# Late weight steps three products later, and scores in tiles of 64 rows in four periods: an attention and feed-forward kernel on one core

## The chip, the core and the metric

The kernel runs on one core of one Trainium2 chip. A core has TensorE (PE, matrix products into PSUM; its weight loads are listed as PEld), VectorE (DVE), ScalarE (ACT), GpSimd (POOL) and SyncE (SP, which issues most DMAs). The metric is the device time of one execution in microseconds (us). All inputs and outputs lie in the chip's memory, and one launch computes everything.

## What is computed

Attention in which a query sees only the keys of its own cluster, and then a feed-forward block (ffn) over all tokens:

```python
# q, k, v: (4, 8, 768, 64); centroids: (8, 16, 64); all float32
q_assign = argmax(einsum('bhsd,hcd->bhsc', q_n, c_n), -1)      # the same for k; _n: normalised
mask     = q_assign[:, :, :, None] == k_assign[:, :, None, :]
scores   = where(mask, q @ k.T / sqrt(64), -1e9)
scores   = scores - max(scores, -1)
attn     = exp(scores); attn = attn / (sum(attn, -1) + 1e-9)
x        = (attn @ v), heads side by side: (3072, 512)

h  = x @ w_in                       # w_in: (512, 2048)
sp = maximum(h, 0) + log1p(exp(-abs(h)))
g  = h * erf(sp)
out = g @ w_out                     # w_out: (2048, 512); out: (3072, 512)
```

## The kernel before

**Attention.** Two heads make a pair `p` (16 pairs), one head on partitions 0 to 63 and one on 64 to 127. A pair has two halves of 384 queries and six blocks of 128 keys; a unit `u` is one half against one block of keys, 12 units a pair, 192 in all. The loop at the bottom calls `period(p, i)` 96 times, each for two units. A period issues in order: a step of the maxima for the coming half (`step_ahead(u)`), `products(u)` and `products(u + 1)`, a second step of the maxima in two pieces, `scores(u)`, `scores(u + 1)`, the exponentials (`curve`) on ACT, and for the two units of the period before the sums (`accumulate`) on POOL and the product with v (`attend`) on PE. At the start of every half stands `divide` for the half before: row sums by a product with `minus`, Ln and Exp on ACT, four DVE instructions, and four DMAs to `x_dram`.

`products` multiplies q and k (float32, 64 rows of contraction for each head, and so two row tiles of the array at a time). `scores` adds onto the same PSUM tile what masks and shifts: `qm` and `km` hold, in bfloat16, a one-hot of the cluster and, in row 0 of each head, the negated maximum. Rows 32 to 63 of each head hold the one-hot of the cluster again. `scores` uses rows 0 to 31 of each head, that is, tiles of 32 rows at rows 0 and 64; the second step of the maxima in a period (`behind=True`) uses rows 32 to 63 and 96 to 127, in tiles of 32 rows as well. Maxima are taken one half ahead: `step_ahead(u)` works for unit `u + 6`. So none is left for the last six units (186 to 191, three periods), and in the first period (`u == 0`) they are issued ahead of the period and after its scores.

**The ffn.** A matrix product is done as seven smaller ones over sums and differences of the quarters of its operands ("forms": `left_forms`, `right_forms`). `hidden(n, lot)` makes one half of h for the chunk `n` of 512 tokens: four blocks of seven products, each product of 4 matmul records into a PSUM bank of its own, evicted by the functions that `fresh` lists. Of a block, product 1 is copied by ACT (`first=ae.copy`) and products 2, 6, 7, 5 (twice), 3 and 4 are taken by DVE, in this order. `block` runs, after each product and its evictions, the next `pace` entries of a list `aside_work`, which holds single instructions of other work in the order in which they are to be issued; `finish_aside` issues what is left at the end. Program order is kept on PE, DVE, ACT and POOL.

The banks: six of the pool `psb`, in turn; from the end of the first block on (`finish_attention`, which runs the last `divide`) also the two `turned` tiles of attention, as the seventh and eighth of every eight products.

**The weights.** Each weight step takes 512 columns of a weight matrix, already fetched as 512 KB, and turns them into a float32 array in five parts: `size_and_rest` (ACT, two instructions), `bounded` (DVE), `sign` (ACT), `shifted` (DVE) and `summed` (POOL). `summed` also issues the fetch that uses the freed place. The last ten steps (`N_LATE`, all of `w_out`) run in the ffn. Their first four fetches are issued ahead of `hidden(0, 0)`, into memory that attention held until its last accumulation. Steps 0 to 3 are run beside `hidden(0, 0)` (28 products, `pace` 1, 20 parts), followed by eight POOL instructions that make forms of `w_out` (`out_forms[0]`, `out_forms[1]`); steps 4 to 9 beside `hidden(0, 1)`, together with the gate (softplus and erf on ACT, product on DVE).

Of the kernel before, what the change touches and what calls it, by code (L numbers as in the profile page):

```python
# [20 lines left out]
B, H, S, D = 4, 8, 768, 64  # L21
C = 16
NJ = S // P
Q = 32
# [46 lines left out]
def kernel(  # L71
# [68 lines left out]
    rows = [{nm: const.tile([P, S], F32, name=f"{nm}T{i}") for nm in "qk"} for i in range(2)]  # L140
# [124 lines left out]
    for e in range(2):  # L265
        for n in range(2):
            r = e * D + n * Q
# [50 lines left out]
    def similarities(p):  # L318

        if p >= NPAIR:  # L320
            return
        st = pairs[p]
        st["psim"] = turned[1][:, 0:HW]
        for g in range(4):
            te.matmul(
                st["psim"][2 * C * g : 2 * C * (g + 1)], lhsT=ccT[:, p % HP],
                rhs=st["qk"[g // 2] + "T"][:, (g % 2) * HW : (g % 2 + 1) * HW],
                start=True, stop=True,
            )
# [31 lines left out]
    def masks(p, nm, half, bank, narrow=False, copied_by=ae):  # L361

        if p >= NPAIR:
            return lambda: None
        st = pairs[p]
        cols = slice(half * HW, (half + 1) * HW)
        r, hot = slice(0, D) if nm == "q" else slice(D, P), st["hotT"]
        picked = pick[r, half]
        if narrow:
            r = slice(r.start + Q, r.stop)  # L370
            picked = pick[r, 1]
            hot = hot if half else st["aside"]
        won = bank[:, 0:HW]
        te.matmul(won, lhsT=picked, rhs=hot[r], start=True, stop=True)
        if nm == "q":
            return lambda: ae.activation(out=st["qm"][:, cols], in_=won, func=ACT.Relu)
        if copied_by is ve:
            return lambda: ve.tensor_scalar(
                out=st["km"][:, cols], in0=won, scalar1=BIG, scalar2=nbig, op0=ALU.mult, op1=ALU.add
            )  # L380
        return lambda: ae.activation(
            out=st["km"][:, cols], in_=won, func=ACT.Identity, bias=nbig, scale=BIG
        )
# [34 lines left out]
    def turn(p, h, copies=(ae.copy, ae.copy)):  # L418

        st = pairs[p]  # L420
        pn = turned[h][:, 0:HW].rearrange("p (t n) -> p t n", t=HJ)
        for t in range(HJ):
            for e in range(2):
                cols = slice(e * D, e * D + Q)
                te.matmul(pn[cols, t], lhsT=lowest[h][:, t, cols], rhs=identb, start=True, stop=True)
        for e, copy in zip(range(2), copies):
            r = slice(e * D, e * D + 1)
            copy(out=st["qm"][r, h * HW : (h + 1) * HW], in_=pn[r].rearrange("p t n -> p (t n)"))
        st["shift", h] = True
# [4 lines left out]
    units = [(p, half, j) for p in range(NPAIR) for half in range(2) for j in range(NJ)]  # L434
# [3 lines left out]
    def products(u):  # L438
        p, half, j = units[u]
        if u in sc_of:  # L440
            return
        st = pairs[p]
        sc = sc_of[u] = ps_s.tile([P, 2, 512], F32, name="sc", tag="s")
        for e in range(2):
            r = slice(e * D, (e + 1) * D)
            te.matmul(
                sc[:, e, 0:HW], lhsT=st["kT"][r, j * P : (j + 1) * P],
                rhs=st["qT"][r, half * HW : (half + 1) * HW], start=True, stop=False,
            )

    def scores(u):

        p, half, j = units[u]
        st = pairs[p]
        sc = sc_of[u]
        assert ("shift", half) in st
        for e in range(2):
            r = slice(e * D, (e + 1) * D)
            r = slice(r.start, r.start + Q)
            te.matmul(  # L460
                sc[:, e, 0:HW], lhsT=st["km"][r, j * P : (j + 1) * P],
                rhs=st["qm"][r, half * HW : (half + 1) * HW], start=False, stop=True,
            )

    def curve(u):

        pr = prs[u % NPT]
        sc = sc_of.pop(u)[:, :, 0:HW].rearrange("p e (c x) -> p e c x", c=2)
        ae.activation(out=pr[:, :, :, 0:QW], in_=sc, func=ACT.Exp, scale=D**-0.5)
# [143 lines left out]
    aside_work = []  # L613
# [89 lines left out]
    def idle(n):  # L703
        return [lambda: None] * n
# [39 lines left out]
    def run(work):  # L744
        for _ in work:
            pass
# [3 lines left out]
    def step_ahead(u, behind=False):  # L750
        p, i = divmod(u + NJ, 2 * NJ)
        steps = maxima_step(p, i, behind=behind) if p < NPAIR else iter(())
        if not behind:
            run(steps)
        return steps
# [7 lines left out]
    def period(p, i):  # L763
        u = 2 * NJ * p + 2 * i
        n1, n2 = 2 * p - 1, 2 * p
        early = lambda n: 0 <= n < N_EARLY

        def mask(place):
            which = (MASKS if p else FIRST_MASKS).get((i, place))
            if which:  # L770
                return masks(p + 1, *which, turned[0 if i in (0, 5) else 1], place > 1, ve if i == 0 else ae)
            return lambda: None

        if u > 0:
            for which in turns if i in (0, 3) else ():
                turn(*which)
                turns.remove(which)
            step_ahead(u)
        mask(0)()
        next(part[0], None)  # L780
        if i == 5:
            next(routing[0], None)
        if i == 0 and p:
            run(routing[0])
        if u == 2:
            next(routing[0])
        products(u)
        products(u + 1)
        mask(1)()
        second = step_ahead(u + 1, True) if u > 0 else iter(())  # L790
        next(second, None)
        scores(u)
        next(second, None)
        if i:
            next(second, None)
        next(part[0], None)
        scores(u + 1)
        later = mask(2)
        if i == 0:
            later()  # L800
            later = lambda: None
            next(second, None)
        if i == 3:
            similarities(p + 2)
            routing[0] = choose(p + 2, sc_of[u + 1][:, 0], True)
        curve(u)
        later()
        curve(u + 1)
        if u == 0:
            step_ahead(1)  # L810
            similarities(1)
            routing[0] = choose(1, turned[0])
            next(routing[0])
            next(routing[0])
            vectors(1, "q")
            vectors(1, "k")
        if i == 0 and early(n1 - 1):
            bounded(n1 - 1)
            shifted(n1 - 1)
            sign(n1 - 1)  # L820
        elif i == 1 and early(n1):
            size_and_rest(n1)
        elif i == 3 and early(n1):
            bounded(n1)
            sign(n1)
        elif i == 5 and early(n2):
            rest(n2)
        for _ in range(min(len(forms), FORMS.get(p, {}).get(i, 0))):
            forms.pop(0)[0]()
        if i == 3:  # L830
            next(routing[0], None)
            if early(n1):
                shifted(n1)
            for _ in range(2):
                next(routing[0], None)
        elif i == 1:
            load(p + 1, "v", v, vp)
            if p == 0:
                run(routing[0])
                transposes(2, "q")  # L840
        elif i == 2:
            transposes(p + 2, "k")
        elif i == 4:
            vectors(p + 2, "k")
            vectors(p + 2, "q")
        elif i == 5:
            transposes(p + 3, "q")
        if u > 0:
            if i == 1 and early(n1 - 1):
                summed(n1 - 1)  # L850
            elif i == 4 and early(n1):
                summed(n1)
            for w in (u - 2, u - 1):
                accumulate(w)
            if i % HJ == 1 and p in POOL_FORMS and forms:
                forms.pop(0)[1]()
            for w in (u - 2, u - 1):
                attend(w)
            if i % HJ == 0:
                part[0] = divide(u - 1)  # L860
                next(part[0])
        if i == 3 and early(n2):
            size(n2)
# [71 lines left out]
    u = len(units)  # L935
# [30 lines left out]
    def all_weights(lo, hi):  # L966
        return sum((weights(n) for n in range(lo, hi)), [])

    out_forms = [right_forms(ge, *w_out_parts(f, 2)) for f in range(0, HF, 2)]
# [10 lines left out]
            del a[:1], b[:1]  # L980
        return work

    aside_work += all_weights(0, 4) + out_forms[0] + out_forms[1]
    hidden(0, 0, {0: finish_attention})
    finish_aside()
    aside_work += together(idle(2) + gates(0, 0, (0,)), all_weights(4, N_LATE))
# [56 lines left out]
```

## Time and profile before

Three runs took 995.52, 995.58 and 996.94 us; the median is 995.58. The profiled execution took 995.37 us, and its span, from the first instruction to the last, is 993.7 us.

| what | value |
|---|---|
| attention, from the start to the last product with v on PE | to 408.4 us |
| first ffn step, `hidden(0, 0)`, PE | 408.4 to 434.5 us |
| second ffn step, `hidden(0, 1)`, PE | 434.5 to 458.65 us |
| busy of DVE, ACT, POOL in 408.4 to 435.3 (26.90 us) | 19.36, 14.24, 13.40 us |
| busy of DVE, ACT, POOL in 435.3 to 458.6 (23.30 us) | 21.15, 18.11, 10.38 us |
| score passes of 32 rows, 384 columns: number, mean | 384, 326 ns |
| DMA landing of a late weight step (512 KB), median | 3.3 us (into `g_more`), 4.7 us (into `osb`) |

In the lists of the profile a line gives the start, the duration, the engine, the operation with output and inputs by their names in the program, the tile of the array (`64*128` is 64 rows by 128 columns), the shape, and the number of instructions that were put together; in brackets stands how long the engine had been idle and what ended that. The end of a matmul is modelled, so two starts are compared rather than an end and a start. A matmul in float32 appears as two records. All instructions bear one line number (L62), since a helper issues them, so the tile names tell them apart. `sc` is the tile of products and scores, `wide` that of the maxima, `bank` an ffn bank.

### The profile page before, as it was taken

The page shows a single profiled execution, that of the slowest core. Times are in us where ns is not written, and L with a number is a line of the kernel's source. Part 1 is how long each engine was busy: PE and PEld are TensorE (multiplying, and loading weights), DVE is VectorE, ACT ScalarE, POOL GpSimd, SP SyncE. Part 2 cuts the span into 40 slices and gives each one's busy share as a digit, 9 for nine tenths or more (in the row PEclk, how much of TensorE's full clock was granted, in tenths as well). Part 3 has the DMA queues.
Part 4 walks back from the last instruction along what each step waited for, and adds up shares of the span by engine and source line. Part 5 has one row for each costly group of instructions (what it writes and reads, how often), then busy time and mean ns, then how long its engine had stood idle before and what let it go on. Part 6 is the DMA issues. An engine that isn't in the chain of part 4 may idle for free.

```text
span 993.7 us, 20557 instructions
## 1 busy us (share of the span) xinstructions
PE 985.4 (99%) x8362; PEld 738.8 (74%) x8362; DVE 708.4 (71%) x1361; ACT 488.2 (49%) x659; POOL 350.6 (35%) x237
## 2 busy tenths in 40 slices
PE   8999999999999999999999999999999999999998
PEld 3555555555555555688888888888888888888887
DVE  8888888888888886779676564756475647655653
ACT  3777777777776665575432414150505050505050
POOL 1688888787888888562400000000000000000000
PEclk9999999999999999999999999999999999999999
DMA  9444444444444210321000100010001000000001
GB/s 220 83 109 109 111 112 112 110 114 110 93 88 108 51 34 18 114 97 61 1 22 22 43 1 22 22 43 1 22 22 43 1 21 22 1 1 22 22 1 42
DMA packets 147294, 55.88 MB, mean 56 GB/s; under 512 B 128640, under 2 KB 137088, under 8 KB 147200
## 3 DMA queue, kind: packets, MB, share of 16 engines
q1 hardware_dynamic: 144848, 54.29, 21.5%
q8 instruction: 65, 1.06, 0.4%
q10 hardware_dynamic: 2352, 0.30, 0.2%
q14 instruction: 29, 0.24, 0.1%
HBM read 41.98 MB, written 12.58 MB: 55 GB/s over the span
## 4 chain that ended last, share of the span: by engine, by line
PE 95%; DVE 1%; POOL 1%; DMA 1%; issue 0%; SPq 0%; ACT 0%; ACTq 0%; DVEq 0%; POOLq 0%
PE bank L62 43%; PE turned L62 31%; PE sc L62 16%; PE wide L62 6%; POOL more_out L62 1%; DVE nmx L62 1%; DMA g_more<-in_moe_w_out_dram 0%; DMA in_k<-in_k_dram 0%; SPq L62 0%; DMA in_q<-in_q_dram 0%; DVE kT L62 0%; DVE sims L62 0%; POOL x_more L62 0%; DVE qT L62 0%; ACT pr L62 0%
## 5 line engine op out<-in xcount | busy, mean ns | idle before, releaser
L62 POOL TENSOR_TENSOR more_out<-more_out,pr 128x768 f32<-128x768 f32 x128 | 217.2, 1697 | 18.6 <-ACT pr L62 10.1
L62 DVE TENSOR_REDUCE nmx<-wide 128x2 f32<-128x768 f32 x189 | 180.5, 955 | 48.2 <-PE wide L62 47.2
L62 ACT ACTIVATE pr<-sc 128x768 f32<-128x768 f32 x192 | 148.9, 812 | 94.6 <-PE wide L62 78.6
L62 PE MATMUL turned<-pr,in_v 128*32 128x194 f32 x3072 | 145.5, 330 | 0.0
L62 PEld LDWEIGHTS turned<-pr,in_v 128*32 128x32 f32 x3072 | 91.5, 109 | 51.2 <-issue 21.3
L62 DVE TENSOR_TENSOR g<-bank,g 128x256 f32<-128x256 f32 x222 | 89.7, 422 | 52.9 <-PE bank L62 46.3
L62 PE MATMUL bank<-x_own,w_in 128*128 128x256 f32 x424 | 104.7, 380 | 0.9 <-DVE g L62 0.9
L62 PE MATMUL bank<-w_out,g 128*128 128x256 f32 x448 | 103.1, 379 | 0.0
L62 PE MATMUL sc<-qT,kT 64*128 64x384 f32 x528 | 98.3, 486 | 0.0
L62 PEld LDWEIGHTS bank<-w_out,g 128*128 128x128 f32 x448 | 85.1, 190 | 11.6
L62 PEld LDWEIGHTS bank<-x_own,w_in 128*128 128x128 f32 x424 | 80.3, 190 | 12.7 <-DVE g L62 1.3
L62 DVE TENSOR_TENSOR osb<-bank,osb 128x256 f32<-128x256 f32 x87 | 35.5, 421 | 72.8 <-ACT osb L62 25.4
L62 ACT COPY g<-bank 128x256 f32<-128x256 f32 x28 | 10.4, 372 | 152.9 <-PE bank L62 148.4
L62 ACT ACT_TABLE_LOAD x48 | 61.6, 1283 | 45.7 <-DVE g L62 45.1
L62 PE MATMUL bank<-x_more,more_in 128*128 128x256 f32 x296 | 76.0, 379 | 0.0
L62 POOL TENSOR_TENSOR more_out<-pr,pr 128x768 f32<-128x768 f32 x32 | 60.1, 1879 | 28.1 <-ACT pr L62 28.1
L62 PEld LDWEIGHTS <-qv 64*128 64x128 bf16 x384 | 26.9, 93 | 53.1 <-issue 37.0
L62 PEld LDWEIGHTS sc<-qT,kT 64*128 64x128 f32 x528 | 50.0, 187 | 21.3 <-ACT inv L62 2.3
L62 PE MATMUL wide<-kv,qv 64*128 64x384 bf16 x378 | 64.0, 328 | 1.3 <-DVE nmx L62 0.6
L62 PE MATMUL bank<-more_out,g_more 128*128 128x256 f32 x272 | 64.3, 379 | 0.0
L62 DVE TENSOR_TENSOR g<-a_s,g 128x512 f32<-128x512 f32 x96 | 62.5, 689 | 1.4 <-ACT a_s L62 1.4
L62 PE MATMUL wide<-km,qm 64*128 64x384 bf16 (+1 forms) x378 | 62.5, 327 | 0.0
(172 smaller groups left out, 1669.9 us busy)
## 6 DMA issues: line engine op xcount, KB each, us to landing
x_own<-in_moe_w_in_dram SPq DMA_DIRECT2D x13, 512.0 KB, 4.0
in_v<-in_v_dram SPq DMA_DIRECT2D x32, 192.0 KB, 3.0
x_dram<-more_out SPq DMA_DIRECT2D x128, 48.0 KB, 1.7
x_own<-x_dram SPq DMA_DIRECT2D x6, 1024.0 KB, 5.2
out_dram<-osb SPq DMA_DIRECT2D x23, 256.0 KB, 2.0
in_k<-in_k_dram SPq DMA_DIRECT2D x59, 96.0 KB, 2.6
in_q<-in_q_dram SPq DMA_DIRECT2D x58, 96.0 KB, 2.6
g_more<-in_moe_w_out_dram SPq DMA_DIRECT2D x6, 512.0 KB, 3.3
```

The costliest lines, as they stand in the source:

```text
L62: ins = getattr(self.engine, name)(*args, **kw)
```

## The change

Two edits. The first puts three empty entries ahead of the list for `hidden(0, 0)`, so that each part of the weight steps 0 to 3 and each of the eight POOL instructions is issued three products later; the last three are then issued after the last product, by `finish_aside`. The second gives `scores` the number of rows as an argument: 64 rows of each head (`D`) for the first two units and for the last six, 32 rows (`Q`) for all others. With 64 rows the mask's part of the sum is added twice (rows 32 to 63 repeat it); row 32 of each head holds a zero in `qm`, and the shift is added once.

```diff
-    def scores(u):
+    def scores(u, rows=Q):
...
-            r = slice(r.start, r.start + Q)
+            r = slice(r.start, r.start + rows)
             te.matmul(
                 sc[:, e, 0:HW], lhsT=st["km"][r, j * P : (j + 1) * P],
...
+        rows = D if u == 0 or u + NJ >= len(units) else Q
-        scores(u)
+        scores(u, rows)
...
-        scores(u + 1)
+        scores(u + 1, rows)
...
-    aside_work += all_weights(0, 4) + out_forms[0] + out_forms[1]
+    aside_work += idle(3) + all_weights(0, 4) + out_forms[0] + out_forms[1]
     hidden(0, 0, {0: finish_attention})
     finish_aside()
```

## The prediction

> **What bounds the kernel now.** I read the page first: which engine has no gaps, and what the chain that ended last is made of.
>
> ```profile
> PE 985.4 (99%) x8362; PEld 738.8 (74%) x8362; DVE 708.4 (71%) x1361; ACT 488.2 (49%) x659; POOL 350.6 (35%) x237
> PE 95%; DVE 1%; POOL 1%; DMA 1%; issue 0%; SPq 0%; ACT 0%; ACTq 0%; DVEq 0%; POOLq 0%
> ```
>
> PE is the bound nearly everywhere. The change can only take time out of PE's own stream or out of the few places where PE waits. The table of waits, for PE alone, lists six, and one of them lies in the first ffn step:
>
> ```profile
> PE bank L62 <- DVE g L62: 0.9, 1, 0.9
> ```
>
> The chain of waits from 408 us to 424 us shows who makes it:
>
> ```profile
> 409.57 2.02 POOL more_out L62
> 411.59 0.02 issue
> 411.61 3.73 DMA g_more<-in_moe_w_out_dram
> ...
> 415.60 0.67 ACT w_out L62
> ...
> 416.30 0.04 DVE w_out L62
> ...
> 416.64 0.43 DVE g L62
> 417.07 0.04 issue
> 417.11 4.58 PE bank L62 x20
> ```
>
> The last accumulation on POOL ends at 411.59 and frees the attention's memory. Only then is late weight step 0 fetched. Its `size` on ACT starts when the fetch has landed, its `bounded` on DVE waits for `size`, and the evictions of the PSUM banks stand behind `bounded`. The timelines of DVE and PE there:
>
> ```profile
> 412.06 0.41 DVE L62 TENSOR_TENSOR g<-bank,g 128x256 f32<-128x256 f32 x1
> 416.30 0.43 DVE L62 TENSOR_SCALAR w_out<-w_out 128x512 f32<-128x512 f32 x1 [3.83 <-ACT w_out L62]
> ...
> 415.08 1.13 PE L62 MATMUL bank<-x_own,w_in 128*128 128x256 f32 x4
> 417.11 1.13 PE L62 MATMUL bank<-x_own,w_in 128*128 128x256 f32 x4 [0.90 <-DVE g L62]
> 418.08 1.03 PE L62 MATMUL bank<-x_more,more_in 128*128 128x256 f32 x4
> ```
>
> DVE has evicted product 2 (412.06), then stands 3.83 us. PE runs on until the six banks are used up: the second product of the second block needs the bank of product 6, which DVE frees at 417.07. For the scores, the timeline of PE with the maxima beside, and without:
>
> ```profile
> 385.18 1.45 PE L62 MATMUL sc<-qT,kT 64*128 64x384 f32 x8
> 386.47 0.33 PE L62 MATMUL wide<-kv,qv 64*128 64x384 bf16 x2
> 386.73 0.33 PE L62 MATMUL sc<-qm,km 32*128 32x384 bf16 x2
> ...
> 403.69 1.56 PE L62 MATMUL sc<-qT,kT 64*128 64x384 f32 x8
> 405.19 0.50 PE L62 MATMUL sc<-qm,km 32*128 32x384 bf16 x4
> 405.61 2.83 PE L62 MATMUL turned<-pr,in_v 128*32 128x194 f32 x64
> ```
>
> From the products to a 64-row pass takes 386.47 - 385.18 = 1.29 us, but to a 32-row pass 405.19 - 403.69 = 1.50. Where the maxima run, the 32-row form is free, since scores and maxima share the array (at 386.73 the two run as one); in the last three periods nothing shares it.
>
> **What the Trainium skill says.** "TensorEngine Tiling (Array Packing)", Key Properties: changing the tiling mode, not just the tile, drains the engine. The trace agrees: a pair of bf16 passes is 0.17 us ahead of the next pair of its mode (365.21 to 365.38), but 0.26 us ahead of one of another mode (386.47 to 386.73), so a switch is about 0.10 us. "TensorE: Matmul & The Clock Gate", section on the array as 16 sub-arrays: ACT and DVE are strict FIFO; the 3.83 us above, with finished banks waiting behind one instruction, is that. "GPSIMD Engine Reference", specifications: POOL shares SBUF interfaces with VectorE, contended by VectorE's two-port modes and by two SBUF inputs. The trace agrees: a 512-wide subtraction of two SBUF operands on DVE took 0.68 us with POOL idle (453.33) and 2.17 beside POOL's accumulations (405.78). This matters for a rival.
>
> **The weight steps, three products later.** Nothing is removed or added; 20 step parts and 8 POOL forms move from products 1 to 28 of this step to products 4 to 31, and since it has 28 products the last three POOL forms are issued after it. The fetch stays where it was. Gone: `bounded` of step 0 now stands behind the evictions of products 6, 7 and 5, not before them.
>
> Size of the stall: 408.38 to 410.21 is two products after a mode change, 1.83 us, so 0.865 a product and 0.10 for the change. The product that began at 415.08 would have released the next at 416.04; it began at 417.11, and 417.11 to 418.08 is 0.97, again 0.10 over. Cost: 1.07 + 0.10 = 1.17 us.
>
> What is late next, in times of before with PE's gain applied (0.3 from the scores by 408 us, then 1.17). DVE evicts products 2, 6, 7 and 5 from 412.06 to about 413.9 and waits in `bounded` to about 416.6, then products 3 and 4, done by about 417.0 and 417.3. Their banks are needed by the fifth product of the second block at 418.2 and the sixth at 419.1: over 1 us to spare. Then the division, which uses both `turned` banks. Its Ln on ACT stood behind `size_and_rest` of step 1 (0.60 and 0.58 us); these move past it, so Ln begins at about 417.9 (before: 419.14) and the DVE part, four instructions, runs about 418.7 to 420.45 (before 419.96 to 421.71). PE needs `turned` 0 at 420.0 (freed at 419.05) and `turned` 1 at 420.8: 0.4 us to spare, before 0.7 (422.39). Thin, but no wait.
>
> Every queue moved past: on SP, the fetch for step 4, released by `summed` of step 0, now comes behind the four x stores of the division; about 420.4 + 4 x 0.435 = 422.2 instead of 419.67, landing near 425.9 at 3.7 us, and its `size` is due near 428.3 (before 429.77); beyond those 2.4 us ACT would stand, and the gate of the second step with it. POOL: `summed` of step 3 and then the forms follow the end of DVE's catching up, which comes earlier because nothing of the first block is left over; I work out 429.3 for the forms instead of 430.05. They are read from 462.11 on. In the second step DVE is nearly full (21.15 of 23.30 us busy), and the eviction ending 458.31 frees a bank that PE takes at 458.65, so 0.34 us to spare. That chain hangs on ACT's gate, which waits for the last eviction of the first step (ACT idle 2.81 us before 435.14), so it moves forward with PE. I take the full 1.17; bounds 0.5 to 1.2.
>
> **The scores in 64 rows.** Eight calls of 192, two passes each: 16 matmuls, same columns, same weights' columns. In the three last periods products and scores become one mode: one switch less. The scores' two pairs still take one after the other (0.17 apart before too), and from a 64-row pair to a 128x32 pass is 0.26 us (20.44 to 20.70), as from a 32-row pair (398.29 to 398.55). Gain 0.10 each, 0.30 in all. The rest of the 0.21, some 0.11, lies in the first pair of products after a switch (396.62 to 397.05, 0.43 instead of 0.32) and stays. Bounds: 0, if the drain only moves, to 0.21 each. In the first of them PE then reaches the row sums at 399.78, and POOL's accumulation ends at 399.75: up to 0.05 may be given back. In the first period PE saves a switch too, but the chain there is DVE's (transpose from 19.83 to 20.81, maximum at 20.84, and on to 23.84), and the second score pass waits for DVE's copy at 19.81 anyway: 0, at most 0.2 if that cover failed.
>
> **Sum.** 1.17 + 0.25 = 1.42 us. The profiled execution took 995.37 us (993.7 of span and 1.67 around it): 993.95. The median of the runs shown is 0.21 higher (995.58): 994.16. I say 994.1.
>
> **Rivals.** A partial refund (0.13): the thin `turned` 1 margin or the banks of products 3 and 4 fail, because the fetch lands a microsecond later or the division is slower. For: 0.4 us to spare is within what I can work out. Against: ACT and DVE free it 1.2 us earlier. It would leave half: 994.8. A larger gain (0.10): both ends of the excess go and the first period counts, 4 x 0.21 + 1.17 = 2.0: 993.5. Against: the 0.11 sits ahead of the products, which are unchanged.
>
> Slower (0.09): the second step. If POOL's weight sums and forms really come three products (2.6 us) later, they fall on DVE's SBUF-only instructions, each of which can then wait out a POOL instruction of 1.28 us, as `bounded` at 456.53 did (1.45 instead of 0.42). With y of delay at the eviction of 458.31 PE loses y - 0.34; it decides against the change from y = 1.8, and three such collisions (3.84) give 995.58 - 1.42 + 3.5 = 997.7. Against: POOL's order there is set by DVE's catching up, not by the product count, and DVE has 1.15 us idle before 442.00.
>
> **How the numbers follow.** Forecast as above 0.68. About 0.2%, 2.0 us, is what can be told from no change. Faster by more: half of the larger gain and 0.09 of the forecast's tail, 0.14. Slower by more: 0.09. Within: 0.77. Range: from the larger gain, 993.3, to a refund of nearly all, 995.5; beyond it lies the slower case and a little at each end.
>
> **What would show it.** Right: no PE wait on DVE near 416 us; DVE's wait for ACT now after the eviction of product 5; the products to scores distance 1.40 instead of 1.50 in the last three periods; ffn products from about 408.1 us; period 0 unchanged to its next maxima at 23.84. Wrong: a PE wait on `turned` near 420.5, or on a bank near 457; or a span shorter by less than 1 us with none of these.

## The result, and the profile after

| | median, us | range, us | runs |
|---|---|---|---|
| before | 995.75 | 995.27 to 996.94 | 22 |
| changed | 994.41 | 993.83 to 995.40 | 22 |

The ratio of changed to before is 0.9986, with a 95% interval of 0.9979 to 0.9992: 1.34 us less, by the medians; the interval reaches from 0.8 to 2.1 us less. Forecast were 994.1 us, 1.42 less than the median of the first three runs of before (995.58), and a range of 993.3 to 995.5. Over 22 runs the median of before is 0.17 us higher than over those three.

The profiled execution of the changed kernel took 994.52 us with a span of 992.8, so only 0.85 less than that of before. The two executions do not start alike: the turn of the first maxima on PE, ahead of anything that was changed, begins at 18.69 us instead of 18.36, and the products of period 93, the first of the last three, at 396.99 instead of 396.62. So the two traces are compared by distances between starts on PE, not by absolute times.

The page's fourth part (shares of the chain that ended last, by engine) and the table of waits for PE, of the changed kernel:

```profile
PE 98%; DVE 1%; DMA 0%; issue 0%; ACT 0%; SPq 0%; DVEq 0%
```

```profile
PE turned L62 <- DVE alleps L62: 2.4, 1, 2.4
PE wide L62 <- DVE nmx L62: 0.6, 3, 0.2
PE wide L62 <- ACT km L62: 0.6, 1, 0.6
PE turned L62 <- DVE lowest L62: 0.2, 1, 0.2
```

PE's share of the chain went from 95% to 98%, and the wait of a bank on DVE is gone from the list. What is left of PE's waits lies in the first 25 us, but for one of 0.2 us on `nmx` between 100 and 200 us. Now the places themselves, first the timeline of PE in the changed kernel:

```profile
396.99 1.56 PE L62 MATMUL sc<-qT,kT 64*128 64x384 f32 x8
...
403.90 1.56 PE L62 MATMUL sc<-qT,kT 64*128 64x384 f32 x8
405.29 0.49 PE L62 MATMUL sc<-qm,km 64*128 64x384 bf16 x4
405.71 2.83 PE L62 MATMUL turned<-pr,in_v 128*32 128x194 f32 x64
408.48 1.99 PE L62 MATMUL bank<-x_own,w_in 128*128 128x256 f32 x8
...
415.18 1.99 PE L62 MATMUL bank<-x_own,w_in 128*128 128x256 f32 x8
...
433.42 1.03 PE L62 MATMUL bank<-x_own,w_in 128*128 128x256 f32 x4
...
456.73 1.03 PE L62 MATMUL bank<-x_more,w_in 128*128 128x256 f32 x4
457.70 3.72 PE L62 MATMUL bank<-w_out,g 128*128 128x256 f32 x16
461.26 1.89 PE L62 MATMUL bank<-more_out,g_more 128*128 128x256 f32 x8
```

Products to scores take 405.29 - 403.90 = 1.39 us (before 1.50), and the first two products of the second ffn block stand in one line of eight records (415.18), with no stall between them. But there is something new: the first product of the projection starts at 457.70, where 456.73 + 0.865 = 457.59 was due, and from it to the next line, two products later, are 461.26 - 457.70 = 3.56 us, 0.10 more than before (462.11 - 458.65 = 3.46). These 0.10 us, which a product takes longer when it starts after a wait, are called a restart below. The list of waits for PE does not have this wait, because the end of the product before it is modelled at 457.76, after the start. The page of the changed kernel shows it at the weight loads of these products, with DVE as releaser; the page of before names none there:

```profile
L62 PEld LDWEIGHTS bank<-w_out,g 128*128 128x128 f32 x448 | 85.0, 190 | 11.9 <-DVE g L62 0.4
```

DVE, in the same kernel's timeline:

```profile
412.41 2.33 DVE L62 TENSOR_TENSOR g<-bank,g 128x256 f32<-128x256 f32 x5
416.76 0.43 DVE L62 TENSOR_SCALAR w_out<-w_out 128x512 f32<-128x512 f32 x1 [2.02 <-ACT w_out L62]
...
440.96 1.56 DVE L62 TENSOR_SCALAR w_out<-w_out 128x512 f32<-128x512 f32 x1 [0.88 <-ACT w_out L62]
...
457.24 0.41 DVE L62 TENSOR_TENSOR g<-g,bank 128x256 f32<-128x256 f32 x1
```

Five evictions (products 2, 6, 7 and twice 5) now run ahead of `bounded` of step 0, which then waits 2.02 us with nothing urgent behind it. The eviction that ends at 457.65 is taken to be the one that PE waits for at 457.70: the start follows it by 0.05 us, as 417.11 followed an eviction that ended at 417.07 before.

The same starts in the timeline of PE before:

```profile
396.62 1.56 PE L62 MATMUL sc<-qT,kT 64*128 64x384 f32 x8
...
408.38 1.99 PE L62 MATMUL bank<-x_own,w_in 128*128 128x256 f32 x8
...
434.48 1.03 PE L62 MATMUL bank<-x_own,w_in 128*128 128x256 f32 x4
...
458.65 3.62 PE L62 MATMUL bank<-w_out,g 128*128 128x256 f32 x16
462.11 1.89 PE L62 MATMUL bank<-more_out,g_more 128*128 128x256 f32 x8
```

The account, in starts on PE: from the products of period 93 to the first ffn product (the three last periods), from there to the first product of the second step, from there to the first of the projection, and the restart after it.

| kernel | last three periods | first step | second step | restart | sum |
|---|---|---|---|---|---|
| before | 11.76 | 26.10 | 24.17 | 0 | 62.03 |
| changed | 11.49 | 24.94 | 24.28 | 0.10 | 60.81 |

The periods gave 0.27 us and the first step 1.16; 0.21 went back at the end of the second step; 1.22 us remain. The medians gave 1.34, but with their interval they can't tell 1.22 from the 1.42 that were forecast; the account by places is what tells them apart.

### The profile page after: what moved, and what is told of

Its sections match the earlier page's. It is cut to its first block, busy times and chain, and to the rows that moved or that the text cites. A ratio compares the mean times of both kernels' runs of the same rounds, so it can differ in the third digit from the quotient of the medians.

```text
span 992.8 us, 20557 instructions
## 1 busy us (share of the span) xinstructions
PE 985.6 (99%) x8362; PEld 739.5 (74%) x8362; DVE 709.1 (71%) x1361; ACT 488.1 (49%) x659; POOL 350.6 (35%) x237
## 4 chain that ended last, share of the span: by engine, by line
PE 98%; DVE 1%; DMA 0%; issue 0%; ACT 0%; SPq 0%; DVEq 0%
PE bank L62 44%; PE turned L62 32%; PE sc L62 16%; PE wide L62 6%; DVE nmx L62 1%; DMA in_q<-in_q_dram 0%; DVE sims L62 0%; DVE kT L62 0%; DVE qT L62 0%; DVE km L62 0%; DVE turned L62 0%; DVE nbig L62 0%; ACT qm L62 0%; DVE osb L62 0%; SPq L62 0%
```

## The experiments

Two explanations stood at this point, and each run below says what either expects. Theory A: the fetch of weight step 0 waits for POOL's last accumulation, and with it the whole chain over ACT, DVE and POOL in the first step keeps its time whatever PE does; and the new wait comes from POOL, which is late with the forms of `w_out`. Theory B, the rival: the edits simply add, and DVE is full in the second step with or without POOL.

### The weight steps alone

The kernel before with this one line:

```diff
-    aside_work += all_weights(0, 4) + out_forms[0] + out_forms[1]
+    aside_work += idle(3) + all_weights(0, 4) + out_forms[0] + out_forms[1]
```

> The kernel before with the three empty entries alone, scores in 32 rows everywhere. Theory A (the fetch of weight step 0 hangs on POOL's last accumulation, and everything behind it on ACT, DVE and POOL keeps that time whatever PE does): the first ffn step takes 24.94 us on PE instead of 26.10, the last three periods stay at 11.76, and the wait of 0.1 us that the changed kernel has at the first projection product is gone, since PE arrives 0.27 us later against the same DVE: in all 1.16 us less than before, nearly as much as both edits together (1.22 inside the trace). Theory B (the two edits simply add): 0.95 us less, with the wait still there.

Measured: 994.55 us against 995.74, ratio 0.9988 (0.9982 to 0.9995). On PE: 11.76, 24.93 and 24.18 us, no restart, sum 60.87, which is 1.16 less than before. The timeline of PE at the projection, in this kernel:

```profile
455.70 1.03 PE L62 MATMUL turned<-x_own,more_in 128*128 128x256 f32 x4
...
457.43 3.62 PE L62 MATMUL bank<-w_out,g 128*128 128x256 f32 x16
```

Two products from 455.70 to 457.43 are 1.73 us, and 3.62 is the undisturbed duration of the sixteen records: no wait. So in the traces this edit alone brings as much as both, but for 0.06 us, as theory A had it.

### The scores alone

The changed kernel with the line above as it was in the kernel before, so that only the scores in 64 rows are left of the change.

> The changed kernel without the three empty entries: only the scores in 64 rows. Theory A: the last three periods take 11.49 us instead of 11.76, but PE then waits 0.27 us longer for the bank of product 6, whose time is set by POOL, fetch, ACT and DVE: first ffn step 26.35 instead of 26.10, total gain 0.0 (at most 0.1). Theory B: the 0.27 us stay, and the stall is still 1.17.

Measured: 995.86 us against 995.74, ratio 1.0001 (0.9993 to 1.0009). On PE: 11.48, 26.35 and 24.17, sum 62.00, 0.03 less than before. The timeline of PE in the first step of this kernel:

```profile
415.12 1.13 PE L62 MATMUL bank<-x_own,w_in 128*128 128x256 f32 x4
417.39 1.13 PE L62 MATMUL bank<-x_own,w_in 128*128 128x256 f32 x4 [1.14 <-DVE g L62]
```

From 415.12 to 417.39 are 2.27 us, before 2.03 (415.08 to 417.11): PE comes earlier and waits longer, for a bank whose time POOL, fetch, ACT and DVE set. What the tiles of 64 rows save in the last periods is lost again 9 us later, but for 0.03 us, as theory A had it.

### The POOL forms earlier

On the changed kernel. The weight steps keep their places; the forms no longer follow step 3 but go with the parts of steps 2 and 3 (they read what steps 0 and 1, and the early steps, have made).

```diff
-    aside_work += idle(3) + all_weights(0, 4) + out_forms[0] + out_forms[1]
+    def both(a, b):
+        return lambda: (a(), b())
+    forms_8, parts = out_forms[0] + out_forms[1], all_weights(2, 4)
+    aside_work += idle(3) + all_weights(0, 2)
+    aside_work += [both(w, f) for w, f in zip(parts, forms_8)] + parts[8:]
```

> The changed kernel with the eight POOL forms issued right after weight step 1, each together with a part of steps 2 and 3, so that POOL is done some 3 us earlier. Theory A (the new wait at the first projection product comes from POOL: its forms end late, summed of step 4 follows, and DVE's bounded of step 5 waits for it): bounded of step 5 ends about 0.6 us earlier against PE, no wait there, second step 24.17 us instead of 24.28 and no restart after it, 0.2 us less in all than the changed kernel. Theory B (DVE is simply full in the second step): the wait stays, 24.28.

Measured: 994.26 us against 995.74, ratio 0.9985 (0.9979 to 0.9992). On PE: 11.49, 24.94 and 24.17, no restart, sum 60.60: 0.21 less than the changed kernel and 1.43 less than before, as theory A had it. So the 0.27 us of the scores count in full here, beside the 1.16 of the weight steps. By the times alone it can't be told from the changed kernel (intervals overlap nearly whole); the traces tell them apart. POOL and then DVE in the timeline of the changed kernel:

```profile
430.58 1.27 POOL L62 TENSOR_TENSOR more_out<-w_out 128x512 f32<-128x512 f32 x1
...
439.70 1.28 POOL L62 TENSOR_TENSOR more_out<-more_out,w_out 128x512 f32<-128x512 f32 x1
440.94 1.30 POOL L62 TENSOR_TENSOR w_out<-w_out,g_more 128x512 int32<-128x512 int32 x1
```

and in the timeline of the kernel with the forms earlier:

```profile
436.85 1.29 POOL L62 TENSOR_TENSOR w_out<-w_out,osb 128x512 int32<-128x512 int32 x1
440.04 1.29 POOL L62 TENSOR_TENSOR w_out<-w_out,g_more 128x512 int32<-128x512 int32 x1 [1.91 <-ACT g_more L62]
...
440.44 1.18 DVE L62 TENSOR_SCALAR w_out<-w_out 128x512 f32<-128x512 f32 x1 [0.69 <-ACT w_out L62]
```

POOL's sum of step 4 and `bounded` of step 5 before:

```profile
441.60 1.30 POOL L62 TENSOR_TENSOR w_out<-w_out,g_more 128x512 int32<-128x512 int32 x1 [1.02 <-ACT g_more L62]
...
442.00 1.18 DVE L62 TENSOR_SCALAR w_out<-w_out 128x512 f32<-128x512 f32 x1 [0.85 <-ACT w_out L62]
```

In the changed kernel POOL goes from the last form (439.70) straight into the sum of step 4 (440.94), and `bounded` of step 5, ready at 440.96, is held to the end of that sum: 1.56 us instead of the 0.42 of an undisturbed one. With the forms earlier POOL has been idle 1.91 us, the sum starts earlier, and `bounded` takes 1.18; that the sum of step 3 (436.85) now comes late does no harm. On PE's clock, which counts from the first product of the second step, `bounded` ends 0.41 us earlier than in the changed kernel; 0.6 was expected. That is enough to take the wait away. The four kernels on that clock, in us:

| kernel | sum of step 4 starts | `bounded` of step 5 ends | eviction ahead of the projection ends |
|---|---|---|---|
| before | 7.12 | 8.70 | 23.83 |
| weight steps alone | 7.15 | 8.75 | 23.87 |
| changed | 7.52 | 9.10 | 24.23 |
| changed, forms earlier | 7.11 | 8.69 | 23.82 |

Of these four only the changed kernel has the sum late against PE, and the 0.4 us pass through `bounded` to the eviction 15 us later. With the weight steps alone POOL goes straight from the last form into the sum as well, but it does so 0.37 us earlier against PE: 0.27 because PE comes later there, and 0.10 because the fetch of step 0 landed sooner in that execution (ACT waits 3.62 us for it, 3.71 in the changed kernel, 3.61 before, 3.75 with the forms earlier). With a landing as before, the eviction of the changed kernel would end at 24.13, an estimate, and PE, due at 24.17, would wait about 0.01 us instead of 0.11. One execution was traced, and whether the others of the changed kernel have this wait is not shown. With the forms earlier it is gone although the fetch landed last of all there.

### Seven products later

The changed kernel with seven empty entries, `idle(7)`, in place of three.

> The changed kernel with seven empty entries instead of three. Theory A: the first step stays at 24.94 us without a wait, but POOL's sum of step 3 now comes with the 27th product, the forms about 2.2 us later, and DVE's bounded of step 5 as much later: PE waits about 2 us in all for banks in the second step, which takes some 26.2 us, and the kernel is slower than before by about 0.7 us. Theory B (POOL has no part in it): 24.3 us in the second step and the time of the changed kernel.

Measured: 995.62 us against 995.74, ratio 0.9997 (0.9989 to 1.0005). On PE: 11.48, 24.94, 25.43 and a restart of 0.10, sum 61.95. So the second step does pay, and the kernel loses nearly all that it had won; but it pays 1.26 us and not 2, and is no slower than before. POOL and DVE in this kernel's timeline, and PE at the projection:

```profile
434.33 1.27 POOL L62 TENSOR_TENSOR more_out<-w_out 128x512 f32<-128x512 f32 x1
...
445.60 3.18 POOL L62 TENSOR_TENSOR w_out<-w_out,g_more 128x512 int32<-128x512 int32 x2
...
440.91 0.47 DVE L62 TENSOR_SCALAR w_out<-w_out 128x512 f32<-128x512 f32 x1 [0.87 <-ACT w_out L62]
...
446.11 1.52 DVE L62 TENSOR_SCALAR w_out<-w_out 128x512 f32<-128x512 f32 x1
447.55 0.41 DVE L62 TENSOR_TENSOR g<-bank,g 128x256 f32<-128x256 f32 x1
447.89 1.44 DVE L62 TENSOR_TENSOR g<-a_s,g 128x512 f32<-128x512 f32 x1
...
458.81 1.56 PE L62 MATMUL bank<-w_out,g 128*128 128x256 f32 x6 [0.38 <-DVE g L62]
```

The forms start at 434.33, 3.75 us later than in the changed kernel (2.2 had been expected), but `bounded` of step 5 (440.91) is not held until they are through: it meets the end of one form and takes 0.47 us. The price falls mostly on later instructions that start some 0.5 us after a POOL instruction (446.11 and 447.89, beside the two sums listed as one from 445.60 on); alone they take 0.42 and 0.68 us, so they lost 1.10 and 0.76. What a DVE instruction waits for is the POOL instruction in flight, not POOL's queue, and so the delay depends on which instructions meet, not on the whole shift.

### One product later

The changed kernel with one empty entry, `idle(1)`.

> The changed kernel with one empty entry instead of three. Theory A (DVE's bounded of step 0 always ends when the fetch lets it, 417.1 us in the changed kernel, and what counts is which evictions stand behind it and what ACT does ahead of the division): products 7, 5, 3, 4 stand behind it, PE waits some 0.55 us for the bank of product 7, and Ln of the division comes 1.15 us later behind step 1, so that the turned banks are free only just in time and PE may wait again, 0 to 0.35 us. First step 25.6 to 26.0 us, about 1 us longer than with three entries; in all 0.2 to 0.6 us less than before. Theory B (any shift that takes product 6 out from behind it is enough): 24.94 us.

Measured: 995.07 us against 995.53, ratio 0.9996 (0.9988 to 1.0004). On PE: last periods 11.49 us, first step 25.77, second 24.17, sum 61.43, which is 0.60 less than before. The times alone do not tell this kernel from before. The timeline of PE in the second block of this kernel:

```profile
415.12 2.00 PE L62 MATMUL bank<-x_own,w_in 128*128 128x256 f32 x8
417.31 1.13 PE L62 MATMUL bank<-x_more,more_in 128*128 128x256 f32 x4 [0.19 <-DVE g L62]
...
420.86 1.03 PE L62 MATMUL turned<-x_more,w_in 128*128 128x256 f32 x4
421.99 1.13 PE L62 MATMUL turned<-x_own,w_in 128*128 128x256 f32 x4
```

Two waits, with a restart each: 0.46 us for the bank of product 7 (417.31 instead of 416.95, and 0.10) and 0.36 for `turned` 1 (421.99 instead of 421.73, and 0.10); together they are the 0.83 us by which the step is longer than with three entries. About 0.55 and up to 0.35 had been expected. So both chains of the prediction can end PE's wait: the evictions behind `bounded`, and the division behind ACT's weight parts.

### Sixty-four rows everywhere

The changed kernel with 64 rows in every period.

```diff
-        rows = D if u == 0 or u + NJ >= len(units) else Q
+        rows = D
```

> The changed kernel with scores in 64 rows in every period. If the 32-row form is free where the second step of the maxima shares the array, each of the 92 other periods pays one pair of passes more (0.17 us) and one change of mode more (0.10): 0.27 x 92 = 25 us, near 1019 us. If only the pass were lost it would be 16 us, near 1010; if sharing brought nothing, about 994.

Measured: 1031.43 us against 995.53, ratio 1.036 (1.0341 to 1.0379); the span is 37.2 us longer than the changed kernel's, where 25 were expected. The timeline of PE in two periods of this kernel, one without and one with a mask in it:

```profile
387.94 0.33 PE L62 MATMUL wide<-kv,qv 64*128 64x384 bf16 x2
388.11 0.33 PE L62 MATMUL sc<-qm,km 64*128 64x384 bf16 x2
388.36 0.34 PE L62 MATMUL wide<-km,qm 32*128 32x384 bf16 x2
388.63 0.34 PE L62 MATMUL sc<-qm,km 64*128 64x384 bf16 x2
388.90 1.52 PE L62 MATMUL turned<-pr,in_v 128*32 128x194 f32 x32
...
392.66 0.34 PE L62 MATMUL sc<-qm,km 64*128 64x384 bf16 x2
392.93 0.33 PE L62 MATMUL turned<-hotT,pick 32*128 32x384 bf16 x1
393.19 1.52 PE L62 MATMUL turned<-pr,in_v 128*32 128x194 f32 x32
```

Where attention starts in the kernel before, after the maxima at 386.47:

```profile
387.16 1.52 PE L62 MATMUL turned<-pr,in_v 128*32 128x194 f32 x32
```

Maxima to attention take 388.90 - 387.94 = 0.96 us; before it was 387.16 - 386.47 = 0.69. That is the 0.27 expected, 24.8 us over 92 periods. The rest I had overlooked: 44 masks are made with 32 rows too (30 from `hotT`, 14 from `aside`), and in the kernel before they ran beside the scores at no cost (scores at 363.17, mask at 363.18, attention at 363.43: the same 0.26 us as from 386.90 to 387.16 without a mask). Each is now a pass and a switch of its own, 393.19 - 392.93 = 0.26 us, and 11.4 us if all 44 cost as much. Together these are 36.2 of the 37.2 us; the last microsecond was not traced.

### The first period back to 32 rows

The kernel with the forms earlier, and 64 rows for the last three periods only (`rows = D if u + NJ >= len(units) else Q`).

> The kernel with the forms earlier, with the first period back at 32 rows, so that only the last three periods have 64. If the first period is worth nothing (DVE sets its end): the same time as with both, 994.3 us, and from the product of the first period to the maxima of the next 5.2 us in both. If it counts: 0.1 to 0.2 us more.

Measured: 994.23 us against 995.53, ratio 0.9987 (0.9980 to 0.9993). From the products of the first period to the maxima for unit 9, beside the scores of the next: 18.68 to 23.91, 5.23 us; with 64 rows there, 18.52 to 23.73, 5.21. The first period is worth nothing that can be told from 0.02 us.

## Why the prediction was right, and where a step failed

**The stall.** The prediction was right in place, cause and size: 1.17 us were worked out, 1.16 measured with both edits (26.10 to 24.94) and 1.17 with this edit alone (26.10 to 24.93). What is late next was right too. `turned` 1 was freed at 421.03 and taken at 421.33, 0.3 us to spare where 0.4 had been worked out, and the run with one entry shows it ending. Slips in the sums there had no effect: 1.47 us off the times of before, PE's next starts are 418.3, 419.2, 420.1 and 420.9, not 418.2 to 420.8; and the evictions ahead of `bounded` wait for PE's products, so that they ended at 414.74 (414.4 by the clock of before) and not at 413.9. Of the results, 994.16, 994.87 and 993.57 were rounded down by up to 0.07 us.

**The scores.** The size was right in its place, 0.27 us where 0.25 had been taken, and so was the part that stays: products to scores 1.39 us, forecast 1.40. The first product pair after the switch keeps its extra time (0.42 us, before 0.43). The row sums came 0.04 us later after the attention products than before (398.80 to 400.17 instead of 398.55 to 399.88), the refund by POOL that was foreseen. The first period gave nothing, as said. Wrong was to count the 0.25 in full in the sum. Alone it is worth 0.03 us of trace, beside the weight steps 0.06, and 0.27 only once the forms are issued earlier: the chain from POOL's last accumulation on doesn't move with PE. POOL gained next to nothing in the last periods. It began the half's first sum 0.11 us earlier on the common clock, took 1.92 us instead of 1.82 for it, and ended its last at 411.94, exactly the 0.36 by which the execution began later.

**The step that failed** is "POOL: `summed` of step 3 and then the forms follow the end of DVE's catching up, which comes earlier because nothing of the first block is left over; I work out 429.3 for the forms instead of 430.05." They began at 430.58; even with the later start of that execution taken off, they are 0.9 us later than worked out. With the weight steps alone they began at 430.05, in an execution that starts the first step 0.06 us earlier than before, so that edit moved them by nothing that can be told. DVE was not through earlier: its timeline has `shifted` of step 3 at 428.78 (before 428.26), 0.16 us later by the clock of before. It stood less, 2.02 us for `size` and 1.10 for the Ln and Exp of the division instead of 3.83 for `size` alone; but `shifted` now stands behind two products more, 21 evictions since 412 us instead of 19, the first five of them waited for PE, and one `bounded` (424.34) took 1.14 us beside a POOL sum. From it follows the second error, "so it moves forward with PE": ACT's gate did (434.07 instead of 435.14, 1.43 earlier by the common clock), but DVE's chain behind it gained only about 1.0, since it ran into POOL. On PE's clock the eviction ended 0.40 us later than before (24.23 us instead of 23.83, in the table above). Of the 0.34 us to spare 0.05 lie between an eviction's end and PE's start (457.65 to 457.70); the other 0.29 were used up, and the 0.11 that are left, with a restart, are the 0.21. Some 0.10 of the delay is the later landing of the fetch in that execution, so in others less than 0.21 may have gone back.

**The rivals.** The slow one had the right place and mechanism, but the effect was far smaller than it needed: its y, the delay of the eviction, was 0.40 us, where 1.8 would have turned the sign. The run with seven entries shows it at work, 1.36 us with the restart, and even there it does no more than undo the gain. Its sum of "three such collisions (3.84)" was too much even for that run, where the two that cost most took 1.10 and 0.76 us. The partial refund came, but from this place and not from the `turned` banks or the evictions of products 3 and 4. The larger gain did not come: the 0.11 us sit ahead of the products and stayed.

**A queue** was judged wrong without effect: the fetch for step 4 was to come behind the four x stores on SP. SP issued it at 420.15, ahead of them (421.07).

**The size.** 1.42 were forecast and 1.22 found within the trace, 1.34 by the medians. The difference to the trace is the 0.21 of the second step, less the 0.02 that the periods gave more than counted. That the medians lie nearer to the forecast than the trace does is no merit of it.

## What to carry to other kernels

A wait in an in-order queue is removed best by moving what waits, not by speeding up what comes before: time saved ahead of a chain that hangs on something else (here a fetch behind POOL's last accumulation) is only waited off later, as the scores alone showed. When work is moved later, follow it to the end of the queue it shares with others: here the cost came 40 us later, from POOL forms that ended too late for DVE's fullest stretch, and it went away when the forms alone were issued earlier. And ask of an instruction's shape what runs beside it: tiles of 32 rows cost a switch (0.10 us) where they are alone, but where maxima and masks share them, giving them up cost 37 us.

## What the runs showed of the hardware

Two things I had not expected at this strength. The DVE instruction `bounded`, with one input, in SBUF (0.42 us alone), is held when it starts while a POOL instruction runs: in the changed kernel (424.34, 435.68, 440.96, 455.87), with the forms earlier (440.44) and with seven entries (440.91) it ended 0.28 or 0.29 us after that instruction, whenever it had started. In the four cases of the changed kernel it took 1.14 to 1.56 us; evictions out of PSUM beside the same POOL work (437.10) kept their 0.41. And a product of PE that starts after a wait for a bank takes 0.09 to 0.10 us longer to the next start: so it was after seven waits of 0.11 to 1.31 us in five of these kernels. After the one of 0.11 us (457.70), which PE's list of waits doesn't have, that nearly doubles the price. The weight load of such a product starts together with it (457.70 for both), where before it started 0.21 us ahead (458.44 for 458.65); that the 0.10 us come from there is likely, but no run tests it.
